# First attention of a fused kernel: tiles of 512 tokens, two changes of the array's form a group, and division by columns

## The chip, the cores and the metric

The kernel runs on one core of a Trainium2 chip, in one launch. The metric is the device time of that launch in microseconds, as the median of several executions. TensorE (PE) multiplies, VectorE (DVE), ScalarE (ACT) and GpSimd (POOL) do the elementwise work, SyncE (SP) issues the DMAs.

## What is computed

Attention in two steps over 32 inducing vectors, then two layers of a multilayer perceptron. N = 12480 tokens, C = 128, hidden width 2048:

```
def mab(q, kv):
    s = scale * (q @ kv.T);  s = s - s.max(-1)
    a = exp(s);  a /= a.sum(-1) + 1e-09
    return a @ kv
h = mab(inducing, x)                 # first attention: 32 x 128
x = mab(x, h)                        # second attention: 12480 x 128
h1 = x @ w_in;  g = maximum(h1, 0) + alpha * minimum(h1, 0);  x = g @ w_out
h2 = maximum(x @ w2_in, 0);  out = (h2 * h2) @ w2_out
```

The four weight matrices arrive as 64-bit floats and are turned into 32-bit floats on the chip, bit by bit.

## The kernel before, in words

The order of all work is written out by hand: each engine executes its instructions in the order of the program's lines, and SP issues the DMAs in that order too, with at most eight of them in flight.

**First attention** (lines 119 to 411). x is cut into 30 tiles of 416 tokens (104 partitions of 4 tokens), four tiles to a group, so that there are eight groups, the last of two tiles. `load_x(g)` (L119) loads a group in pairs of tiles, into four buffers `xg`. One turn of the loop (L332) does for group g:

- `scores` (L245): four matmuls against the inducing vectors, each on its own 32 columns of the array. Such matmuls use the array in another form than the full-width ones
- `transpose_x(g + 1)` (L231): 16 full-width transposes of the next group, into four PSUM banks; the copies to `xT` (L239) go to ACT and DVE in turn
- `maxima`, `exps`, `sums`: the running maximum on DVE (L268, L270), the exponentials on ACT (L280), the running sum
- `values1(g - 1)` (L303): 16 matmuls of 32 columns each; `add_values` adds them to `h_run`
- `transpose_e(g)` (L294): four full-width transposes of the exponentials, copied to `eT` by ACT (L301)
- one step of the conversion of a weight piece: `load_w` loads 512 KB into one of four buffers `raw`; `convs[k]` turns it into floats by two ACT instructions (L164, L167), two on DVE (L171, L175) and one on POOL (L176). Pieces 0 to 3 are `w_in`, 4 to 7 `w_out`

So the array changes its form four times a group. **The tail** (L367 to L415) ends the last group, brings the four running maxima together (L379 to L391), weighs the parts by `wgt` (L394), and makes `hT`, the transposed 32 x 128 result, as `h_run` times `sel` (L410). Here the sum of the weights is taken first, and its reciprocal goes into `sel` (L408):

```
    nc.vector.tensor_scalar(sel, same, wgt, den, op0=ALU.mult, op1=ALU.mult)
    b = y1_bank()
    nc.tensor.matmul(b[:, :P], h_run, sel, start=True, stop=True)
    nc.scalar.copy(hT, b[:, :P])
```

The four `transpose_w_in` (L360: four full-width transposes of `w_in`, then an ACT copy to `wiT`, L365) lie between these steps, and so does the vector `alpha` (L368 to L370).

**Start of the second part** (L514 to L535). `first` is the second attention of tile 0: scores (L432), a transposition on DVE (L440), maximum and difference (L445, L446), the exponentials on ACT (L449), sum, reciprocal, product (L454 to L458), back (L462), and a spread over partitions (L486, L493, L495). `make_w1s` multiplies `hT` by `w_in` (L505). The first matmul of the main loop (`l1_a`, L570) needs both.

**Main loop** (L718): 480 steps, one for each of 30 tiles and 16 pieces of 128 hidden units, with ten matmuls of 128 x 416 in a step. The conversions of `w2_in` and `w2_out`, the second attention of the later tiles, and the stores lie between the steps by a table (`plan`). The conversions follow at fixed steps, so the main loop starts when `hT` is there and works at a slower pace in its first steps.

Of the kernel before, what the change touches and what calls it, by code (L numbers as in the profile page):

```python
# [9 lines left out]
F32 = mybir.dt.float32  # L10
# [3 lines left out]
AF = mybir.ActivationFunctionType  # L14
ALU = mybir.AluOpType
AX = mybir.AxisListType

T, PT, R = 416, 104, 4  # L20

Q = 4

# [2 lines left out]
def attention_then_two_mlps(ctx: ExitStack, tc, x, inducing, w_in, w_out, alpha, w2_in, w2_out, out):  # L26
# [3 lines left out]
    nc = tc.nc  # L30
    _, N, C = x.shape
# [1 line left out]
    DFF = w_in.shape[1]  # L33
    P = 128
    NCH = DFF // P
    assert N % T == 0 and PT * R == T
    NT = N // T
    scale = 1.0 / math.sqrt(C)
    groups = [list(range(a, min(a + Q, NT))) for a in range(0, NT, Q)]

    keep = ctx.enter_context(tc.tile_pool(name="keep", bufs=1))
    att = ctx.enter_context(tc.tile_pool(name="att", bufs=1))
# [14 lines left out]
    def free_bank():  # L57
        turn[0] += 1
        return ms_bank() if turn[0] % 2 or main_loop else y2_bank()
# [13 lines left out]
    def st_tile(name, shape):  # L73
        return st.tile(shape, F32, name=name, tag=name)


    ident = st_tile("ident", [P, P])
    make_identity(nc, ident)

    same = st_tile("same", [P, P])  # L80
# [16 lines left out]
    def xt_cols(t):  # L97
        return xT[:, t * T : (t + 1) * T]
# [18 lines left out]
    x_t = {}  # L117

    def load_x(g):  # L119
        n = len(groups[g])  # L120
        t = st.tile([PT, Q, R, C], F32, name="xg", tag="xg", bufs=4)
        k = 2 if g and n > 1 else 1
        for a in range(0, n, k):
            t0 = groups[g][a]
            nc.sync.dma_start(
                out=t[:, a : a + k],
                in_=x[0, t0 * T : (t0 + k) * T, :].rearrange("(t p r) c -> p t r c", p=PT, r=R),
            )
            if g == a == 0:
                nc.sync.dma_start(out=ind, in_=inducing)  # L130
        x_t[g] = t
# [89 lines left out]
    for g in range(3):  # L221
        load_x(g)
    nc.sync.dma_start(out=al_raw, in_=alpha.rearrange("(c p) -> c p", p=P))
    load_w("w_in", 0)
    load_x(3)

# [1 line left out]

    def transpose_x(g):  # L231
        evac = []
        for i, t in enumerate(groups[g]):
            b = x_banks[i % 2]()
            for r in range(R):
                nc.tensor.transpose(b[:, r * PT : (r + 1) * PT], x_t[g][:, i, r, :], ident[:PT, :PT])  # L236
            copy = nc.vector.tensor_copy if i % 2 else nc.scalar.copy
            evac.append(
                lambda t=t, b=b, copy=copy: copy(  # L239
                    xt_cols(t).rearrange("c (p r) -> c p r", r=R), b[:, :T].rearrange("c (r p) -> c p r", r=R)  # L240
                )
            )
        return evac

    def scores(lhsT, tiles):  # L245
        b = free_bank()
        for i, t in enumerate(tiles):
            nc.tensor.matmul(
                b[i * M : (i + 1) * M, :T], lhsT, xt_cols(t), start=True, stop=True,
                tile_position=(0, i * M),  # L250
            )
        return b


    nm, e, f, s_g, eT, hb = {}, {}, {}, {}, {}, {}
    size = [len(tiles) * M for tiles in groups]
    last = len(groups) - 1

    def small(name):
        return att.tile([P, 1], F32, name=name, tag=name, bufs=2)  # L260
# [1 line left out]
    def maxima(g, b):  # L262
        n = size[g]
        top = small("top")
        nm[g] = small("nm")
        if n < P:
            nc.vector.tensor_copy(nm[g], nm[g - 1])
        nc.vector.reduce_max(top[:n], b[:n, :T], axis=AX.X)  # L268
        if g:
            nc.vector.scalar_tensor_tensor(  # L270
                nm[g][:n], top[:n], -scale, nm[g - 1][:n], op0=ALU.mult, op1=ALU.min
            )
        else:
            nc.vector.tensor_scalar_mul(nm[g][:n], top[:n], -scale)

    def exps(g, b):
        n = size[g]
        e[g] = st.tile([P, T], F32, name="e", tag="e", bufs=2)
        s_g[g] = small("s_g")
        nc.scalar.activation(e[g][:n], b[:n, :T], AF.Exp, bias=nm[g][:n], scale=scale, accum_out=s_g[g][:n])  # L280
# [12 lines left out]

    def transpose_e(g):  # L294
        n = size[g]
        b = y1_bank()
        own = e[g].rearrange("n (p r) -> n r p", r=R)
        for r in range(R):
            nc.tensor.transpose(b[:PT, r * P : r * P + n], own[:n, r], ident[:n, :n])
        eT[g] = st.tile([PT, R, P], F32, name="eT", tag="eT", bufs=2)  # L300
        nc.scalar.copy(eT[g][:, :, :n], b[:PT, : R * P].rearrange("p (r k) -> p r k", r=R)[:, :, :n])  # L301

    def values1(g):  # L303
        hb[g] = y2_bank()
        for r in range(R):
            for i in range(len(groups[g])):
                nc.tensor.matmul(
                    hb[g][i * M : (i + 1) * M, :C], eT[g][:, r, i * M : (i + 1) * M], x_t[g][:, i, r, :],
                    start=(r == 0), stop=(r == R - 1), tile_position=(0, i * M),
                )  # L310

    def add_values(g):
# [8 lines left out]
    def run(fs):  # L321
        for v in fs:
            v()
# [6 lines left out]
    nc.tensor.transpose(b[:, :M], ind, ident[:M, :M])  # L330
    nc.vector.tensor_copy(indT, b[:, :M])
    for g in range(last):  # L332
        cg = g - (last - 6)
        b = scores(indT, groups[g])
        evac = transpose_x(g + 1)
        maxima(g, b)
        evac[0]()
        exps(g, b)
        run(evac[1:2])
        if cg > 1:  # L340
            convs[cg - 2][2]()
        sums(g)
        if cg > 1:
            convs[cg - 2][3]()
        run(evac[2:])
        if cg > 0:
            run(convs[cg - 1][:2])
        if g:
            values1(g - 1)
            add_values(g - 1)  # L350
        transpose_e(g)
        if 0 <= cg < 3:
            load_w("w_in", cg + 1)
        elif cg >= 3:
            load_w("w_out", cg - 3)
        if g + 4 <= last:
            load_x(g + 4)
    load_w("w_out", 3)

    def transpose_w_in(k):  # L360
        b = x_banks[k % 2]()
# [5 lines left out]
    b = free_bank()  # L367
    nc.tensor.transpose(b[:, :NCH], al_raw, ident[:NCH, :NCH])  # L368
    nc.vector.tensor_copy(al, b[:, :NCH])
    nc.vector.tensor_scalar(al1, al, -1.0, 1.0, op0=ALU.mult, op1=ALU.add)  # L370


    b = scores(indT, groups[last])
    values1(last - 1)
    maxima(last, b)
    exps(last, b)
    add_values(last - 1)
    b = free_bank()
    nc.tensor.transpose(b[:1, :P], nm[last], ident)  # L379
    m_all = att.tile([1, M], F32, name="m_all", tag="m_all")  # L380
# [3 lines left out]
    convs[4][2]()  # L384
    sums(last)
    transpose_w_in(0)
    transpose_e(last)
    b = free_bank()
    nc.tensor.matmul(b[:, :1], m_rep.rearrange("o q j -> o (q j)"), ones[:1, :], start=True, stop=True)
    nb = att.tile([P, 1], F32, name="nb_all", tag="nb_all")  # L390
    nc.vector.tensor_copy(nb, b[:, :1])  # L391
    transpose_w_in(1)
    wgt = att.tile([P, 1], F32, name="wgt", tag="wgt")
    nc.scalar.activation(wgt, nm[last], AF.Exp, bias=nb, scale=-1.0)  # L394
    run(convs[5][:2])
    part = att.tile([P, 1], F32, name="part", tag="part")
    nc.vector.tensor_tensor(part, wgt, s_run, op=ALU.mult)
    convs[4][3]()
    values1(last)
    b = free_bank()  # L400
    nc.tensor.matmul(b[:, :1], same, part, start=True, stop=True)
    transpose_w_in(2)
    add_values(last)
    den = att.tile([P, 1], F32, name="den", tag="den")
    nc.vector.tensor_scalar_add(den, b[:, :1], 1e-9)
    nc.vector.reciprocal(den, den)
    sel = st.tile([P, P], F32, name="sel", tag="sel")
# [355 lines left out]
```

## Time and profile before

| | |
|---|---|
| median of 3 runs | 998.91 us (994.25 to 999.48) |
| the profiled execution | 999.72 us, of which the trace's span is 996.8 us |
| busy in the span | PE 98%, ACT 77%, DVE 69%, POOL 56% |
| mean granted TensorE clock | 0.993 of full speed |
| loads up to the main loop | x 6.39 MB, eight weight pieces of 512 KB |

Times in the trace are microseconds from the start of the span. A row of a timeline has start, duration, engine, line, operation, what it writes and reads, the shape and how many; the bracket at the end is the time in which the engine was idle before it, and what ended that. A chain of waits is followed back from the last instruction: each row is a piece of time and what held the kernel up in it.

### The profile page before, as it was taken

To read this page: it belongs to the slowest core of one execution; us is meant where nothing else is said; L and a number is where in the kernel's file an instruction comes from. 1 tells how busy PE (TensorE), PEld (TensorE's weight loads), DVE (VectorE), ACT (ScalarE), POOL (GpSimd) and SP (SyncE) were. 2 spreads that over 40 slices of the span, in tenths; PEclk is the share of its full clock that TensorE was granted. 3 is DMA by queue.
4 is the path that set the end of the run, shared out by engine and by line. 5 is a ranking of instruction groups with operands and counts; after the bars stand their busy time and mean duration, and the time that the engine had idled before them with its cause. 6 is when DMAs were issued, how large, how long until landed. Compare 5 with 4: busy or idle time off the path is not lost.

```text
span 996.8 us, 16261 instructions
## 1 busy us (share of the span) xinstructions
PE 973.7 (98%) x5423; PEld 939.9 (94%) x5423; DVE 684.8 (69%) x1210; ACT 770.4 (77%) x1607; POOL 555.3 (56%) x518
## 2 busy tenths in 40 slices
PE   7879999999999999999999999999999999999998
PEld 5558999999999999999999999999999999999997
DVE  4688776666766667666776667766677666776667
ACT  4569877777887778877787778877787777787776
POOL 1256966555665556655565555655556555565530
PEclk9889999999999999999999999999999999999999
DMA  8715002000020000100001000010000100010001
GB/s 220 200 56 149 1 9 44 10 7 4 10 44 10 10 1 10 44 10 10 3 10 42 10 9 10 10 35 10 9 9 18 27 10 9 10 27 1 10 9 18
DMA packets 66289, 28.42 MB, mean 29 GB/s; under 512 B 54205, under 2 KB 62061, under 8 KB 66205
## 3 DMA queue, kind: packets, MB, share of 16 engines
q1 hardware_dynamic: 66205, 27.39, 12.1%
q8 instruction: 42, 0.69, 0.3%
q14 instruction: 42, 0.34, 0.1%
HBM read 14.80 MB, written 6.39 MB: 21 GB/s over the span
## 4 chain that ended last, share of the span: by engine, by line
PE 91%; DMA 3%; DVE 2%; ACT 2%; issue 1%; POOL 0%; SPq 0%; ACTq 0%; POOLq 0%; DVEq 0%
PE y L582 18%; PE y L581 18%; PE y L580 17%; PE h L582 9%; PE h L581 9%; PE h L580 9%; PE h L570 9%; DMA xg<-in_x_dram 3%; PE ms L432 1%; PE y L597 1%; PE h L236 0%; DMA raw<-in_moe_w_out_dram 0%; ACT g1h L574 0%; DVE mag L175 0%; DVE g1l L576 0%
## 5 line engine op out<-in xcount | busy, mean ns | idle before, releaser
L622 POOL TENSOR_TENSOR g2l<-sq,g2h 128x416 fp32r<-128x416 f32 x456 | 496.2, 1089 | 343.9 <-ACT g2h L620 206.5
L576 DVE SCALAR_TENSOR_TENSOR g1l<-h,g1h 128x416 fp32r<-128x416 f32 x480 | 282.6, 589 | 221.7 <-ACT g1h L574 217.2
L574 ACT ACTIVATE g1h<-h 128x416 fp32r<-128x416 f32 x480 | 248.3, 518 | 132.9 <-PE h L570 129.9
L614 DVE TENSOR_TENSOR sq<-h,r 128x416 f32<-128x416 f32 x480 | 283.6, 591 | 52.2 <-ACT r L612 3.8
L612 ACT ACTIVATE r<-h 128x416 f32<-128x416 f32 x480 | 249.5, 520 | 53.6 <-PE h L582 7.7
L620 ACT CAST g2h<-sq 128x416 fp32r<-128x416 f32 x480 | 255.6, 532 | 2.3 <-DVE sq L614 2.1
L570 PE MATMUL h<-a_s,w1s 128*128 128x416 f32 (+1 forms) x480 | 170.4, 356 | 4.2 <-DVE g1l L576 2.9
L582 PE MATMUL y<-g2l,w2o_hi 128*128 128x416 f32 x480 | 168.7, 351 | 0.3 <-POOL g2l L622 0.3
L582 PE MATMUL y<-g1l,wo_hi 128*128 128x416 f32 x480 | 168.3, 351 | 0.0
L580 PE MATMUL h<-y1h,w2i_hi 128*128 128x416 f32 x480 | 168.1, 350 | 0.2
L582 PE MATMUL h<-y1l,w2i_hi 128*128 128x416 f32 x480 | 167.9, 350 | 0.2 <-DVE y1l L601 0.2
L581 PE MATMUL y<-g1h,wo_lo 128*128 128x416 f32 x480 | 168.0, 350 | 0.0
L581 PE MATMUL h<-y1h,w2i_lo 128*128 128x416 f32 x480 | 168.0, 350 | 0.0
L581 PE MATMUL y<-g2h,w2o_lo 128*128 128x416 f32 x480 | 168.0, 350 | 0.0
L580 PE MATMUL y<-g1h,wo_hi 128*128 128x416 f32 x480 | 167.7, 349 | 0.0
L580 PE MATMUL y<-g2h,w2o_hi 128*128 128x416 f32 x480 | 167.5, 349 | 0.0
L570 PEld LDWEIGHTS h<-a_s,w1s 128*128 128x128 f32 (+1 forms) x480 | 90.5, 189 | 12.0 <-DVE g1l L576 5.7
L580 PEld LDWEIGHTS h<-y1h,w2i_hi 128*128 128x128 f32 x480 | 90.0, 188 | 2.8 <-DVE sq L614 1.4
L580 PEld LDWEIGHTS y<-g1h,wo_hi 128*128 128x128 f32 x480 | 90.3, 188 | 1.0 <-issue 0.5
L582 PEld LDWEIGHTS y<-g2l,w2o_hi 128*128 128x128 f32 x480 | 90.1, 188 | 1.2 <-POOL g2l L622 0.7
L581 PEld LDWEIGHTS y<-g2h,w2o_lo 128*128 128x128 f32 x480 | 90.1, 188 | 0.9 <-POOL w2o_lo L181 0.3
L581 PEld LDWEIGHTS y<-g1h,wo_lo 128*128 128x128 f32 x480 | 90.3, 188 | 0.5
(127 smaller groups left out, 761.4 us busy)
## 6 DMA issues: line engine op xcount, KB each, us to landing
out_dram<-o SPq DMA_DIRECT2D x120, 52.0 KB
xg<-in_x_dram SPq DMA_DIRECT2D x13, 416.0 KB
raw<-in_moe_w_in_dram SPq DMA_DIRECT2D x8, 512.0 KB
raw<-in_moe_w_out_dram SPq DMA_DIRECT2D x8, 512.0 KB
a_s<-a_hi SPq DMA_DIRECT2D x58, 52.0 KB
a_s<-a_lo SPq DMA_DIRECT2D x58, 52.0 KB
xg<-in_x_dram SPq DMA_DIRECT2D x4, 208.0 KB
ind<-in_inducing_dram SPq DMA_DIRECT2D x1, 16.0 KB
```

Of the source, the lines that this page charges most:

```text
L432: nc.tensor.matmul(b[i * M : (i + 1) * M, :w], hT[:, :M], rhs, start=True, stop=True, tile_position=(0, i * M),)
L570: nc.tensor.matmul(b[:, :T], w1s[: a.shape[0], c * P : (c + 1) * P], a, start=True, stop=True)
L574: nc.scalar.activation(hi, b[:, :T], AF.Relu)
L576: nc.vector.scalar_tensor_tensor(lo, b[:, :T], 0.0, f32(hi), op0=ALU.max, op1=ALU.subtract)
L580: nc.tensor.matmul(b, w_hi, hi, start=start, stop=False)
L581: nc.tensor.matmul(b, w_lo, hi, start=False, stop=False)
L582: nc.tensor.matmul(b, w_hi, lo, start=False, stop=stop)
L597: nc.tensor.matmul(b, v_s[: a.shape[0]], a, start=False, stop=True)
L612: nc.scalar.activation(r, b, AF.Relu)
L614: nc.vector.tensor_tensor(sq, b, r, op=ALU.mult)
L620: nc.scalar.copy(hi, sq)
L622: (nc.vector if i >= total - LAG2 else nc.gpsimd).tensor_tensor(lo, sq, f32(hi), op=ALU.subtract)
```

## The change

The first attention gets tiles of its own: 24 tiles of 512 tokens (128 partitions of 4) and one of 192 (96 partitions of 2), that is six full groups and a last one of one tile. The second attention and the main loop keep their tiles of 416.

- **Loads.** `load_x` runs three groups ahead instead of four, and the four `w_in` pieces are issued before the loop, between the groups of x. The `w_out` pieces follow in the loop
- **One turn of the loop.** The ACT part of the conversion comes first, then `scores(g)` and `values1(g - 1)` together (the 32-column matmuls), then maximum and exponentials, then the transposes of x and of e together (the full-width ones). The copies to `xT` come at once behind the transposes
- **Alpha** moves from the tail into the third turn; the conversion of the first `w_out` piece ends inside the loop
- **The tail.** `sel` holds the weights alone. A second matmul gives the denominators as columns (L405 of the changed kernel), and the copy of `hT` becomes a product with their reciprocals on DVE (L413). The copy of the joint maximum (`nb_all`) is gone: ACT reads it from PSUM
- **The `w_in` transposes.** Two stay in the tail, the third moves behind `first[0]`, the fourth behind `second[0]`; they use the `y2` banks
- **Buffers.** `ident` moves to another pool, since it lives longer, and a small tile is made wider, so that the main loop's buffers stay at their addresses

The core of the diff:

```diff
+TILE1 = (512, 128, 4)
+REST1 = (192, 96, 2)
...
+    load_x(0)
+    load_x(1)
+    load_w("w_in", 0)
+    load_x(2)
+    load_w("w_in", 1)
     nc.sync.dma_start(out=al_raw, in_=alpha.rearrange("(c p) -> c p", p=P))
-    load_w("w_in", 0)
     load_x(3)
+    load_w("w_in", 2)
+    load_w("w_in", 3)
...
-            copy = nc.vector.tensor_copy if i % 2 else nc.scalar.copy
+            copy = nc.scalar.copy if i in (0, 3) else nc.vector.tensor_copy
...
     for g in range(last):
...
+        if g:
+            run(convs[g - 1][:2])
+        b = scores(g)
         if g:
             values1(g - 1)
+        maxima(g, b)
+        exps(g, b)
+        if g:
             add_values(g - 1)
+            convs[g - 1][2]()
+        run(transpose_x(g + 1))
         transpose_e(g)
...
+        sums(g)
+        if g:
+            convs[g - 1][3]()
+        if 0 < g and g + 3 <= last:
+            load_x(g + 3)
+        if 0 < g <= 4:
+            load_w("w_out", g - 1)
...
-    nc.vector.tensor_scalar(sel, same, wgt, den, op0=ALU.mult, op1=ALU.mult)
+    nc.vector.tensor_scalar(sel, same, wgt, None, op0=ALU.mult)
+    values1(last)
+    run(convs[5][:2])
+
+    d = ms_bank()
+    nc.tensor.matmul(d[:, :M], s_run.to_broadcast([P, P]), sel[:, :M], start=True, stop=True)
+    add_values(last)
+    den = st.tile([P, M], F32, name="den", tag="den")
+    nc.vector.tensor_scalar_add(den, d[:, :M], 1e-9)
+    nc.vector.reciprocal(den, den)
     transpose_w_in(0)
...
     b = y1_bank()
     nc.tensor.matmul(b[:, :P], h_run, sel, start=True, stop=True)
-    nc.scalar.copy(hT, b[:, :P])
-    transpose_w_in(3)
-    stage1.close()
+    nc.vector.tensor_tensor(
+        hT.rearrange("c (q j) -> c q j", q=Q), b[:, :P].rearrange("c (q j) -> c q j", q=Q),
+        den.unsqueeze(1).to_broadcast([P, Q, M]), op=ALU.mult,
+    )
+    transpose_w_in(1)
...
     make_w1s(0)
+    transpose_w_in(2)
     run(convs[6][:2])
     run(first[1:4])
     split_w1s(0, 0)
     second[0]()
+    transpose_w_in(3)
+    stage1.close()
     make_w1s(1)
```

PE from the last transposes of x to the product that gives `hT`, before (names as in the text; `h_` and `y_` with a number are PSUM banks):

```order
L236 MATMUL h_586<-ident,xg 128x104 x4
L307 MATMUL y_609<-xg,eT 32x128 x16
L299 MATMUL y_627<-ident,e 104x128 x4
L368 MATMUL ms<-ident,al_raw 128x16
L248 MATMUL y_642<-xT,indT 32x416 x2
L307 MATMUL y_645<-xg,eT 32x128 x16
L379 MATMUL ms<-ident,nm 1x128
L364 MATMUL h_681<-ident,w_in_sb 128x128 x4
L299 MATMUL y_687<-ident,e 104x64 x4
L389 MATMUL y_694<-ones,m_rep 128x1
L364 MATMUL h_698<-ident,w_in_sb 128x128 x4
L307 MATMUL y_713<-xg,eT 32x128 x8
```

and with the change:

```order
L248 MATMUL h_556<-ident,xg 128x96 x2
L312 MATMUL y_560<-ident,e 128x128 x4
L260 MATMUL ms<-xT,indT 32x192
L321 MATMUL y_572<-xg,eT 32x128 x16
L385 MATMUL y_599<-ident,nm 1x128
L312 MATMUL y_601<-ident,e 96x32 x2
L392 MATMUL ms<-ones,m_rep 128x1
L321 MATMUL y_620<-xg,eT 32x128 x2
L405 MATMUL ms<-sel,s_run 128x32
L376 MATMUL y_632<-ident,w_in_sb 128x128 x4
L412 MATMUL y_638<-sel,h_run 128x128
```

The last group has one tile of 192 instead of two of 416, and one block of `w_in` transposes stands before the last product where three stood.

ACT from `hT` to the first copy for the main loop (L493 / L497), before:

```order
L411 COPY hT<-y_736 128x128
L365 COPY wiT<-h_739 128x512
L164 ACTIVATE mag<-raw 128x512
L167 ACTIVATE raw<-raw 128x512
L449 ACTIVATE a_760<-a_760 128x128
L512 CAST w1s<-h_755 128x512
L200 CAST wo_hi<-aw 128x512
L493 CAST a_s<-y_784 96x416
```

and with the change:

```order
L377 COPY wiT<-y_641 128x512
L377 COPY wiT<-y_658 128x512
L172 ACTIVATE mag<-raw 128x512
L175 ACTIVATE raw<-raw 128x512
L453 ACTIVATE a_667<-a_667 128x128
L516 CAST w1s<-h_656 128x512
L377 COPY wiT<-y_678 128x512
L208 CAST wo_hi<-aw 128x512
L497 CAST a_s<-y_698 96x416
```

`hT` leaves this queue (DVE writes it), and two more `wiT` copies enter it, one of them ahead of the exponentials of the first tile.

## Rows read from the trace of the kernel before

**Rows 1.** The page: the chain that ended last, share of the span by engine.

```profile
PE 91%; DMA 3%; DVE 2%; ACT 2%; issue 1%; POOL 0%; SPq 0%; ACTq 0%; POOLq 0%; DVEq 0%
```

**Rows 2.** The chain of waits in order of time: start, duration, what.

```profile
2.44 4.34 DMA xg<-in_x_dram
...
27.07 9.68 DMA xg<-in_x_dram
...
36.88 1.62 PE h L236 x8
38.50 1.87 PE y L307 x32
40.36 1.03 PE y L299 x4
41.40 1.55 PE y L248 x8
...
46.16 1.08 DVE al L370
...
52.51 0.96 DVE sel L408
```

**Rows 3.** Windows: stretch, length, busy time of each engine, PE clock, DMA share, GB/s.

```profile
4.00:8.00 4.00, 2.97 (x16) 2.22 (x14) 1.57 (x6) 1.01 (x2) 0.00 (x0) 1.00 0.82 236
...
20.00:30.00 10.00, 8.51 (x120) 5.86 (x120) 5.95 (x16) 7.36 (x19) 1.30 (x1) 1.00 0.97 247
30.00:40.00 10.00, 7.40 (x100) 5.65 (x100) 5.13 (x12) 5.08 (x14) 2.60 (x2) 0.82 0.96 237
...
57.00:63.00 6.00, 3.57 (x15) 1.83 (x13) 5.25 (x11) 3.29 (x7) 3.62 (x4) 1.00 0.23 83
64.00:70.00 6.00, 4.91 (x10) 3.38 (x11) 5.73 (x12) 3.91 (x8) 3.68 (x3) 0.50 0.00 0
```

**Rows 4.** Timeline of the last two groups and the tail, 43 to 53 us.

```profile
43.09 0.59 DVE L268 TENSOR_REDUCE top<-y 128x1 f32<-128x416 f32 x1 [2.31 <-PE y L248]
...
44.05 0.61 ACT L280 ACTIVATE e<-y,nm 128x416 f32<-128x416 f32 x1
44.51 0.41 DVE L171 TENSOR_SCALAR mag<-mag 128x512 int32<-128x512 int32 x1
...
44.91 0.69 PE L299 MATMUL y<-ident,e 128*104 128x128 f32 x4
...
45.10 0.68 DVE L175 SCALAR_TENSOR_TENSOR mag<-raw,mag 128x512 int32<-128x512 int32 x1
...
48.04 0.27 PE L379 MATMUL ms<-ident,nm 128*1 128x128 f32 x1 [0.34 <-DVE nm L270]
...
49.38 0.38 PE L389 MATMUL y<-ones,m_rep 1*128 1x1 f32 x2
...
50.87 0.30 ACT L394 ACTIVATE wgt<-nm,nb_all 128x1 f32<-128x1 f32 x1
...
52.09 1.29 POOL L176 TENSOR_TENSOR w_out_sb<-mag,raw 128x512 int32<-128x512 int32 x1 [4.88 <-DVE mag L175]
```

**Rows 5.** Timeline around the end of the first attention, 53 to 58 us.

```profile
53.90 0.60 PE L364 MATMUL h<-ident,w_in_sb 128*128 128x128 f32 x4
54.10 0.27 ACT L411 COPY hT<-y 128x128 f32<-128x128 f32 x1 [1.13 <-PE y L410]
...
54.54 0.58 ACT L365 COPY wiT<-h 128x512 f32<-128x512 f32 x1 [0.17 <-PE h L364]
...
54.79 1.13 PE L505 MATMUL h<-w_in_sb,hT 128*128 128x512 f32 x2
...
55.02 0.69 ACT L164 ACTIVATE mag<-raw 128x512 f32<-128x512 f32 x1
...
56.16 0.32 ACT L449 ACTIVATE a<-a 128x128 f32<-128x128 f32 x1
...
57.26 0.87 DVE L458 TENSOR_TENSOR a<-a,sm 128x128 f32<-128x128 f32 x1
```

More of the change, by code (lines that the diff above doesn't have):

```diff
@@ L35, in attention_then_two_mlps @@
     NCH = DFF // P
-    assert N % T == 0 and PT * R == T
+    assert N % T == 0
     NT = N // T
@@ L39, in attention_then_two_mlps @@
     groups = [list(range(a, min(a + Q, NT))) for a in range(0, NT, Q)]
+    n1, rest1 = divmod(N, TILE1[0])
+    assert rest1 == REST1[0] and n1 % Q == 0
+    tiles1 = [(i * TILE1[0], *TILE1) for i in range(n1)] + [(n1 * TILE1[0], *REST1)]
+    groups1 = [tiles1[a : a + Q] for a in range(0, len(tiles1), Q)]
     keep = ctx.enter_context(tc.tile_pool(name="keep", bufs=1))
@@ L119, in load_x @@
     def load_x(g):
[L120 to L124, printed above, removed]
+        _, n, p, r = groups1[g][0]
+        t = st.tile([P, Q, TILE1[2], C], F32, name="xg", tag="xg", bufs=4)
+        k = 2 if g else 1
+        for a in range(0, len(groups1[g]), k):
+            t0, kk = groups1[g][a][0], min(k, len(groups1[g]))
             nc.sync.dma_start(
-                out=t[:, a : a + k],
-                in_=x[0, t0 * T : (t0 + k) * T, :].rearrange("(t p r) c -> p t r c", p=PT, r=R),
+                out=t[:p, a : a + kk, :r],
+                in_=x[0, t0 : t0 + kk * n, :].rearrange("(t p r) c -> p t r c", p=p, r=r),
             )
@@ L232, in transpose_x @@
         evac = []
[L233 removed]
+        for i, (t0, n, p, r) in enumerate(groups1[g]):
             b = x_banks[i % 2]()
[L235 to L237 removed]
+            for k in range(r):
+                nc.tensor.transpose(b[:, k * p : (k + 1) * p], x_t[g][:p, i, k, :], ident[:p, :p])
+            copy = nc.scalar.copy if i in (0, 3) else nc.vector.tensor_copy
             evac.append(
[L239 to L240 removed]
+                lambda t0=t0, n=n, r=r, b=b, copy=copy: copy(
+                    xT[:, t0 : t0 + n].rearrange("c (p r) -> c p r", r=r), b[:, :n].rearrange("c (r p) -> c p r", r=r)
                 )
@@ L243, in transpose_x, with scores @@
         return evac
-    def scores(lhsT, tiles):
-        b = free_bank()
-        for i, t in enumerate(tiles):
+    def scores(g):
+        b = ms_bank()
+        for i, (t0, n, _, _) in enumerate(groups1[g]):
             nc.tensor.matmul(
-                b[i * M : (i + 1) * M, :T], lhsT, xt_cols(t), start=True, stop=True,
+                b[i * M : (i + 1) * M, :n], indT, xT[:, t0 : t0 + n], start=True, stop=True,
                 tile_position=(0, i * M),
             )
-        return b
+        return b[:, :n]
     nm, e, f, s_g, eT, hb = {}, {}, {}, {}, {}, {}
-    size = [len(tiles) * M for tiles in groups]
-    last = len(groups) - 1
+    size = [len(tiles) * M for tiles in groups1]
+    last = len(groups1) - 1
     def small(name):
@@ L332, in attention_then_two_mlps @@
     for g in range(last):
[L333 to L347, printed above, removed]
+        if g:
+            run(convs[g - 1][:2])
+        b = scores(g)
         if g:
             values1(g - 1)
+        maxima(g, b)
+        exps(g, b)
+        if g:
             add_values(g - 1)
+            convs[g - 1][2]()
+        run(transpose_x(g + 1))
         transpose_e(g)
[L352 to L358, printed above, removed]
+        sums(g)
[5 more added lines that the diff above has]
+            load_w("w_out", g - 1)
+        if g == 2:
+            b = y2_bank()
+            nc.tensor.transpose(b[:, :NCH], al_raw, ident[:NCH, :NCH])
+            nc.vector.tensor_copy(al, b[:, :NCH])
+            nc.vector.tensor_scalar(al1, al, -1.0, 1.0, op0=ALU.mult, op1=ALU.add)
     def transpose_w_in(k):
-        b = x_banks[k % 2]()
+        b = y2_bank()
         for i in range(4):
@@ L365, in transpose_w_in @@
         nc.scalar.copy(wiT[:, k * 512 : (k + 1) * 512], b)
[L367 to L373, printed above, removed]
+    b = scores(last)
     values1(last - 1)
@@ L383, in attention_then_two_mlps @@
     nc.vector.tensor_copy(m_rep, m_all.unsqueeze(1).to_broadcast([1, Q, M]))
-    convs[4][2]()
+    b = ms_bank()
+    nc.tensor.matmul(b[:, :1], m_rep.rearrange("o q j -> o (q j)"), ones[:1, :], start=True, stop=True)
+    add_values(last - 1)
     sums(last)
-    transpose_w_in(0)
[L387 to L407, printed above, removed]
-    nc.vector.tensor_scalar(sel, same, wgt, den, op0=ALU.mult, op1=ALU.mult)
+    nnm = att.tile([P, 17], F32, name="nnm", tag="nnm")[:, :1]
+    nc.vector.tensor_scalar_mul(nnm, nm[last], -1.0)
+    wgt = att.tile([P, 1], F32, name="wgt", tag="wgt")
+    nc.scalar.activation(wgt, b[:, :1], AF.Exp, bias=nnm)
+    sel = st.tile([P, P], F32, name="sel", tag="sel")
+    nc.vector.tensor_scalar(sel, same, wgt, None, op0=ALU.mult)
[7 more added lines that the diff above has]
+    nc.vector.reciprocal(den, den)
+    transpose_w_in(0)
     b = y1_bank()
     nc.tensor.matmul(b[:, :P], h_run, sel, start=True, stop=True)
-    nc.scalar.copy(hT, b[:, :P])
-    transpose_w_in(3)
-    stage1.close()
+    nc.vector.tensor_tensor(
[3 more added lines that the diff above has]
+    transpose_w_in(1)
     run(convs[5][2:4])
```

36 lines of the change are left out of this document (18 added, 18 removed).

## The prediction

> **What bounds the kernel now.** I read the chain of waits first, by engine [rows 1]: 91% of it is PE. That is the main loop, whose matmuls the diff leaves alone, and whose buffers it keeps where they were. So the change can only move the moment at which the main loop starts. The chain in order of time says what sets that moment [rows 2]. Up to 36.75 us (27.07 + 9.68) the last piece is a transfer of x, so the first attention waits for data and not for an engine. Behind it comes a chain through PE, DVE and ACT that ends with `hT`, written at 54.37 (54.10 + 0.27) [rows 5]. The windows give the rate at which the data come [rows 3]: 236 to 247 GB/s. [...]
>
> Of the main loop one thing counts: whether it follows a shift one for one. Its first steps hang on `hT` through the same order of instructions on ACT, DVE and POOL as before, and the later conversions are tied to steps and not to times. I carry the shift to the end without loss.
>
> **Term 1: when the last full group of x has landed.** Before, that is group 6 of 0 to 7. Ahead of its end lie 28 tiles of 212,992 bytes and three weight pieces of 524,288, 7.54 MB. Now it is group 5 of 0 to 6: 24 tiles of 262,144 bytes and five pieces (all of `w_in` and one of `w_out`), 8.91 MB. The first bytes move at 2.44 [rows 2]. At 237 GB/s [rows 3] 8.91 MB take 37.6 us and land at 40.0; at 247 GB/s [rows 3] they take 36.1 us and land at 38.5; and if a busy share of 0.97 could become 1.00, at 255 GB/s, they land at 37.4. Against 36.75 this is later by 3.3, 1.8 or 0.6. I take 1.2, the middle of the last two, since they come from the stretch with nearly all engines busy, and that is what all of the new stage looks like. The rest of the loop is not on this path: PE works 8.51 of 10 us for 120 instructions, two groups [rows 3], so 4.3 us a group and 5.2 with tiles of 512, while a group of 1.05 MB with a weight piece takes 6.4 us to load at 247 GB/s. On SP the `w_out` piece ahead of group 5 waits for POOL's conversion of the first `w_in` piece, which lands by 13 us, so it holds nothing up. On ACT the conversion steps now stand ahead of the exponentials; the second and third `w_in` piece land behind their groups, which may hold a turn up by 2 us, and the wait for the next group takes that in.
>
> There is a way below 0.6. Between 4 and 8 us, when only x moves, the engines are busy for 0.82 of their time and carry 236 GB/s [rows 3]. 13 of 16 is 0.81, and 104 partitions split into 13 equal parts of 8, 128 into 16. [...] If each engine kept its pace, 16 would carry 236 / 0.82 = 288 GB/s, and the group would land at 33.4. The row from 20 to 30 speaks against that: at 0.97 the engines carry 247, not 279. So I make it a rival, and the term stays at +1.2.
>
> **Term 2: from that landing to `hT`.** Before: 54.37 - 36.75 = 17.6 us. Now, counted from the landing, at the clock of the rows before:
>
> - Eight transposes of 128 columns: 1.62 x 128/104 = 2.0 [rows 2], ends at 2.1 with the gap of 0.13. The transposes of e, 1.03 [rows 2], cover the last copy: 3.1. Four scores of 512 columns: 1.55 x 512/416 = 1.9 [rows 2]: 5.0.
> - Maximum 0.59 x 512/416 = 0.73 [rows 4], with gaps and the small `nm` behind it 6.0. Exponentials 0.61 x 512/416 = 0.75 [rows 4] and the reading of their sums: 6.9. Transposes of e 0.69 [rows 4]: 7.7.
> - DVE has in between the sum of the values, two conversion steps of 0.41 and 0.68 [rows 4] and a running sum. The values of group 4 end on PE at about 6.9 (1.87 behind the scores [rows 2]); these four take 1.7: 8.6. The maximum of the one small tile and two small instructions: 9.2 (an estimate: 0.59 x 192/416 and two of 0.15).
> - PE makes the values of group 5 from 8.35 on, 1.0 (half of 1.87, the clock is back): 9.4. Then `nm` is turned, 0.27 [rows 4]: 9.7. Joint minimum and its copy, 0.5 (an estimate, two small DVE instructions of some 0.25): 10.2. Broadcast 0.38: 10.6. `wgt` 0.30: 10.9 [rows 4].
> - `sel`: it took 0.96 [rows 2], and ended 0.1 behind POOL's conversion (52.09 + 1.29 = 53.38) [rows 4]; without POOL it should cost at most 0.41, as another TENSOR_SCALAR of DVE over 512 columns does [rows 4]. In the new tail POOL's conversion starts at 8.6 and is done at 9.9, so: 11.3.
> - The small matmul of denominators, 0.3; four transposes of `w_in`, 0.60 [rows 5]; the product, 0.46 (an estimate from these); the division on DVE, 0.4 (the copy that it replaces took 0.27): with gaps, `hT` at 13.2.
>
> The gain is 17.6 - 13.2 = 4.4 us. It comes from three places: the alpha instruction (1.08 [rows 2]) out of the way, the last group of one small tile, and fewer transposes and steps between the maximum and the product. The parallel work (denominators, reciprocal) hides behind the transposes of `w_in`; without them it would cost some 0.4.
>
> **Term 3: from `hT` to the main loop.** Here the change costs. The exponentials of the first tile (L449) ended at 56.16 + 0.32 = 56.48 [rows 5], 2.1 behind `hT`. Now ACT has a `wiT` copy ahead of them whose transposes stand on PE behind `make_w1s`. Sum: scores 0.5, L505 1.13, transposes 0.60, copy 0.58, the two conversion steps 0.69 and 0.6, exponentials 0.32 [rows 5]: 4.4, so 2.3 later. Back comes part of the product L458, 0.87 for 128 columns [rows 5], which like `sel` stood in POOL's time; I take 0.4. The fourth block of transposes and its copy lie in time in which ACT waits for the spread on PE (0.60 and 0.58), and I cost them at nothing; if that cover were gone they would cost 0.6. Net +1.9.
>
> **Two changes of form a group instead of four** I cost at nothing: in the loop PE waits for x anyway. At most it is worth the gap of 0.13 us that PE shows ahead of a block [rows 2], twice in the tail.
>
> **The sum** is +1.2 - 4.4 + 1.9 = -1.3 us on the profiled execution's 999.72, that is 998.4. That execution stands 0.8 above the median, so I forecast 997.6 as the median. A measurement of this kernel can tell some 0.5% (5.0 us) from no change, and -1.3 is inside that.
>
> **The rivals.**
>
> - **The clock stays up.** PE fell to half clock twice: after its wait for x, and after 57 to 63, where it was busy for 3.57 of 6 us [rows 3]. From 64 to 70 PE is busy for 4.91 us at 0.50 [rows 3]; at full clock half of that, 2.4 us, is saved. The earlier stretch holds 6.07 us of PE pieces [rows 2], 3.0 at full clock. The two extra transpose blocks behind `hT` make PE busier there, which speaks for it; PE still waits for x, which speaks against the first. One stretch gone: 995.2 (0.20). Both gone: 992.2 (0.07).
> - **Sixteen engines at the pace of thirteen.** Term 1 becomes -3.4 instead of +1.2: 993.0. For it: 0.82 at 236 GB/s. Against it: 247 at 0.97 (0.14).
> - **The bytes set the pace, and there are more of them ahead of the last full group.** The loads come at 237 GB/s or less, since two more weight pieces were moved ahead of it. At 237 the sum is +3.3 - 2.5 = +0.8: 999.7, slower than before. It decides when the group lands later than 39.2; slower by over 0.5% it is only from 44.2 on, a rate of 213 GB/s, which no row shows (0.10 for slower at all, 0.04 of it past the bound, with a third slow stretch of the clock).
> - **The forecast** as it stands: 0.49.
>
> **How the numbers follow.** Faster by over 0.5% (under 993.9) needs both clock stretches gone, or sixteen engines at full pace: 0.21 in all, with a little from one stretch gone and a landing at 37.4, 0.23. Slower by over 0.5%: 0.04. The rest, 0.73, is within 0.5%. The range goes from 991.5, which takes in both ways to be faster, to 1000.5, the pace of 237 GB/s and some tenths of error in terms 2 and 3; what lies outside is the two ways together, and a late landing with a further clock stretch.
>
> **What would show it.** In the profile of the changed kernel the last full group of x should end between 37 and 39 us, `hT` some 13 us later, at about 51, and the first L577 about 8.3 behind `hT`, where it was 6.5. `sel` should take under 0.45. If the group lands before 35, the engines kept their pace. If the first main-loop matmul comes earlier by some 1.3 us but the end moves by another amount, the shift is not carried one for one, and the theory of the main loop is wrong. If no low clock shows behind 55, the clock explains the rest.

## The result and the profile after

The changed kernel takes 987.01 us (median of 4 runs, 985.42 to 988.19) against 999.1 for the kernel before, measured beside it: ratio 0.9889, 95% interval [0.9855, 0.9923]. Measured again it was 986.72 against 997.77, ratio 0.9879 [0.9859, 0.9899]. The forecast of 997.6 and its range from 991.5 were wrong: the gain is 12 us, not 1.3. The profiled execution has a span of 983.6 us (before 996.8).

The page of the changed kernel, first the chain that ended last by engine, then the rate of the DMAs in 40 slices:

```profile
PE 94%; DVE 2%; ACT 2%; DMA 1%; issue 0%; POOL 0%; SPq 0%; ACTq 0%; DVEq 0%
GB/s 329 147 101 55 10 11 34 10 10 10 15 30 10 10 9 18 27 10 10 10 21 25 10 9 10 23 23 10 9 9 30 16 10 10 10 27 1 10 9 19
```

DMA was 3% of the chain [rows 1] and is 1% now: the waits for x have left it. Windows of the changed kernel (columns as in [rows 3]):

```profile
4.00:8.00 4.00, 3.07 (x14) 2.27 (x13) 2.17 (x6) 0.59 (x1) 0.00 (x0) 1.00 0.95 289
12.00:16.00 4.00, 4.00 (x56) 3.02 (x54) 2.22 (x7) 3.60 (x10) 0.00 (x0) 1.00 1.04 403
20.00:24.00 4.00, 4.00 (x60) 3.13 (x58) 3.29 (x9) 3.51 (x8) 1.23 (x1) 1.00 1.06 377
...
28.00:30.00 2.00, 2.00 (x29) 1.80 (x20) 1.63 (x5) 1.65 (x5) 0.56 (x1) 1.00 0.43 119
```

Where 236 to 247 GB/s moved before [rows 3], 289 to 403 move now, and by 28 us the first rush of loads is over. In the windows from 12 and from 20 on PE is busy for all of the 4.00 us. The chain of waits in order of time shows the same:

```profile
2.60 4.85 DMA xg<-in_x_dram
...
15.07 1.90 PE h L248 x16
16.96 0.48 PE y L312 x4
17.44 1.09 PE ms L260 x8
18.53 1.03 PE y L321 x31
...
28.54 1.90 PE h L248 x16
30.43 0.48 PE y L312 x4
30.91 1.26 PE ms L260 x8
```

Behind 7.5 us no load of x stands in it (before, the last one ended at 36.75 [rows 2]). From 10 to 31 us the stage is PE alone, 1.90 + 0.48 + 1.09 + 1.03 = 4.5 us a group. The second load of the last full group completes at 28.75 in the trace, when PE has just begun, at 28.54, to transpose that group's first tiles. The timeline of the end of the first attention and of what follows (it answers to [rows 4, 5]):

```profile
35.63 0.82 DVE L282 SCALAR_TENSOR_TENSOR nm<-top,nm 32x1 f32<-32x1 f32 x1
...
38.27 0.29 DVE L400 TENSOR_SCALAR sel<-same,wgt 128x128 f32<-128x128 f32 x1 [0.39 <-ACT wgt L398]
...
39.75 0.29 DVE L413 TENSOR_TENSOR hT<-y,den 128x128 f32<-128x128 f32 x1
...
43.77 0.30 ACT L453 ACTIVATE a<-a 128x128 f32<-128x128 f32 x1
...
44.84 0.29 DVE L462 TENSOR_TENSOR a<-a,sm 128x128 f32<-128x128 f32 x1
...
47.84 0.84 PE L577 MATMUL h<-a_s,w1s 96*128 96x416 f32 x3 [1.23 <-DVE a_s L499]
```

`hT` ends at 40.04 instead of 54.37 [rows 5], the first main-loop matmul (L577) starts at 47.84 instead of 60.83. From there to the end both take 936 us (935.8 and 936.0).

### The profile page after: what moved, and what is told of

Its sections match the earlier page's. It is cut to its first block, busy times and chain, and to the rows that moved or that the text cites. A ratio compares the mean times of both kernels' runs of the same rounds, so it can differ in the third digit from the quotient of the medians.

```text
span 983.6 us, 16078 instructions
## 1 busy us (share of the span) xinstructions
PE 965.0 (98%) x5341; PEld 936.8 (95%) x5341; DVE 683.1 (69%) x1203; ACT 768.5 (78%) x1600; POOL 555.1 (56%) x518
## 4 chain that ended last, share of the span: by engine, by line
PE 94%; DVE 2%; ACT 2%; DMA 1%; issue 0%; POOL 0%; SPq 0%; ACTq 0%; DVEq 0%
PE y L589 18%; PE y L588 18%; PE y L587 18%; PE h L587 9%; PE h L589 9%; PE h L588 9%; PE h L577 9%; PE h L248 1%; PE ms L260 1%; PE ms L436 1%; PE y L604 1%; ACT g1h L581 1%; PE y L321 1%; DMA xg<-in_x_dram 0%; DVE g1l L583 0%
## 5 line engine op out<-in xcount | busy, mean ns | idle before, releaser
L577 PE MATMUL h<-a_s,w1s 128*128 128x416 f32 (+1 forms) x480 | 170.0, 355 | 4.5 <-DVE g1l L583 2.8
L577 PEld LDWEIGHTS h<-a_s,w1s 128*128 128x128 f32 (+1 forms) x480 | 90.1, 188 | 12.5 <-DVE g1l L583 6.1
L589 PEld LDWEIGHTS h<-y1l,w2i_hi 128*128 128x128 f32 x480 | 90.0, 188 | 0.7 <-DVE y1l L608 0.5
```

Source lines behind the costliest of these rows:

```text
L577: nc.tensor.matmul(b[:, :T], w1s[: a.shape[0], c * P : (c + 1) * P], a, start=True, stop=True)
L589: nc.tensor.matmul(b, w_hi, lo, start=False, stop=stop)
```

## The experiments

**The two halves of the change, each alone.** First the changed kernel with tiles of 416 tokens (the new order, forms and division stay):

```
-TILE1 = (512, 128, 4)
-REST1 = (192, 96, 2)
+TILE1 = (416, 104, 4)
...
-        if g:
+        if 0 < g < 6:
             run(convs[g - 1][:2])
```

> The changed kernel with its first attention back on tiles of 416 tokens (104 partitions); order of the loop, loads between the groups and the new tail stay. Theory A, the gain comes from loading x on 128 partitions: x comes at some 240 GB/s again, hT is written after 48 us, and the time is 994 to 1000 us. Rival B, the gain comes from the order (two changes of form, tail, alpha): hT by 43 us, 986 to 990 us.

Measured: 1002.31 us, ratio to before 1.0040 [1.0021, 1.0059]. The order, the forms and the division without the larger tiles bring no gain; the run is slower. Loads of x are back on its chain (12.76, 11.77 and 9.33 us long), and `hT` ends at 52.05, 2.3 us earlier than before. The main loop starts at 60.96, though, where it was 60.83: from `hT` to there it takes 8.91 instead of 6.46. The changed kernel takes 7.80 there; in this run the clock is at 0.50 from 51 to 54 besides (mean 0.83 from 50 to 60), and the `make_w1s` in that time takes 1.64 instead of 1.06. (The profiled execution took 998.82, the shortest of ten, so its trace does not show all of what the median lost.)

Then the kernel before with nothing but the tiles of 512:

```
-T, PT, R = 416, 104, 4
+T = 416
+TILE1 = (512, 128, 4)
+REST1 = (192, 96, 2)
...
-        t = st.tile([PT, Q, R, C], F32, name="xg", tag="xg", bufs=4)
+        t = st.tile([P, Q, TILE1[2], C], F32, name="xg", tag="xg", bufs=4)
```

> The kernel before with tiles of 512 tokens in the first attention and nothing else changed (its order of loop, loads and tail). Theory A: x comes at over 350 GB/s, hT by 44 us, 987 to 992 us. Rival B: hT after 50 us, 996 us or more.

Measured: 992.43 us, 0.9949 [0.9932, 0.9967]. Here, too, no load of x stands on the chain behind 5.4 us; `hT` ends at 45.85. So the tiles gain 6 us in the old order and 15 in the new one, while the new order loses 4 us with the old tiles and gains 5 with the new ones. The change is not the sum of its parts. With tiles of 416 both orders end the scores of the last full group at nearly the same time (42.95 before, 42.56 in the first of these runs), and what the new order gains from there to `hT` is lost behind it. With tiles of 512 the new order ends them at 32.17 or 33.83 in two executions, the old one at 34.85, and the stretch from there to `hT` is 3.1 us shorter.

**The speed of the loads alone.** Tiles of 512 also change PE's work and the number of groups. This kernel keeps all of the change and only issues each load of x over 128 partitions as two:

```
-            nc.sync.dma_start(
-                out=t[:p, a : a + kk, :r],
-                in_=x[0, t0 : t0 + kk * n, :].rearrange("(t p r) c -> p t r c", p=p, r=r),
-            )
+            src = x[0, t0 : t0 + kk * n, :].rearrange("(t p r) c -> p t r c", p=p, r=r)
+            for u, v in [(0, 104), (104, 128)] if p == P else [(0, p)]:
+                nc.sync.dma_start(out=t[u:v, a : a + kk, :r], in_=src[u:v])
```

> The changed kernel, tiles of 512 tokens and all, with every load of x over 128 partitions issued as two, 104 and 24 partitions, which the loads alone moved at 246 GB/s (0.89 of the engines' time) where one load over 128 moved 388. Nothing else changes. Theory (what the changed kernel gained is the speed of its loads, and without it the 8.91 MB ahead of the last full group set the end as predicted): windows at 230 to 265 GB/s, the first stage waits for x again, the last full group lands 36 to 40 us, hT at 46 to 52 us, 992 to 999 us. Rival (fewer groups, two forms a group and the new end make the gain, and the loads only fill what is free): 986 to 988.5 us.

Measured: 1001.97 us, 1.0028 [1.0011, 1.0045]. A window of it, and the loads on its chain in order of time:

```profile
20.00:30.00 10.00, 7.04 (x70) 5.13 (x69) 4.25 (x9) 4.36 (x9) 1.30 (x1) 0.83 0.97 233
```

```profile
4.87 7.34 DMA xg<-in_x_dram
...
12.23 11.67 DMA raw<-in_moe_w_in_dram
...
23.98 11.23 DMA xg<-in_x_dram
...
35.23 10.33 DMA xg<-in_x_dram
```

The rate is that of before or a little less (233 GB/s here, 247 in the same window before), the last full group lands at 45.55, `hT` ends at 56.34, and the whole gain is gone, with some 3 us more. It was slower than I expected (992 to 999; the bytes that Term 1 left out, below, are the likely reason), but the rival, 986 to 988.5, is out: the gain needs the fast loads. The split also doubles the number of loads. That two loads a tile are not slow of themselves is shown further down, where two loads onto every second partition reach 384 GB/s.

**Why loads over 128 partitions are faster.** Four kernels of loads alone, 2 KB a packet, one stage after the other. In the first, loads over 104, 128, 96, 112, 104 (tiles 512 tokens apart), 120 and 128 (tiles 544 apart) partitions:

```
+    for name, p, step in [("p104", 104, 416), ("p128", 128, 512), ("p96", 96, 384), ("p112", 112, 448),
+                          ("p104_at_512", 104, 512), ("p120", 120, 480), ("p128_at_544", 128, 544)]:
+        stage(name, p, step)
```

> Leaves out the whole computation: it loads x again and again in pairs of tiles, with 104, 128, 96, 112, 104, 120 and 128 partitions a tile, and writes zeros to 128 rows of the output. [...]

Windows of it, one in each of the first four stages and in the last three (columns: stretch, length, DVE, POOL, clock, DMA share, GB/s):

```profile
6.00:16.00 10.00, 0.00 (x0) 0.00 (x0) 1.00 0.86 218
34.00:42.00 8.00, 0.00 (x0) 0.00 (x0) 1.00 1.05 384
52.00:60.00 8.00, 0.00 (x0) 0.00 (x0) 1.00 1.05 282
66.00:80.00 14.00, 0.17 (x1) 0.00 (x0) 1.00 1.07 254
92.00:102.00 10.00, 0.17 (x1) 0.00 (x0) 1.00 0.87 208
114.00:130.00 16.00, 0.17 (x1) 0.00 (x0) 1.00 1.00 230
146.00:152.00 6.00, 0.17 (x1) 0.00 (x0) 1.00 1.03 379
```

The distance of the tiles in memory plays no part (218 and 208; 384 and 379). Nor does the busy share of the engines decide: at 96, 112 and 120 partitions it is 1.00 or more, with 282, 254 and 230 GB/s, and at 128 it is 1.05 and 1.03, with 384 and 379. At 128 the packets take less time. Share x 16 engines x 2048 bytes / rate gives 129 ns a packet at 104 partitions, 122 at 96, and 90 at 128. The second kernel takes other counts and splits:

```
+        ("p64", 256, [(0, 64)]),
+        ("p32", 128, [(0, 32)]),
...
+        ("p64_40", 416, [(0, 64), (64, 104)]),
...
+        ("p104_24", 512, [(0, 104), (104, 128)]),
+        ("p64_64", 512, [(0, 64), (64, 128)]),
```

> Leaves out all of the computation: loads of x alone into eight buffers, stage by stage: 128 partitions in one load, 64, 32, 104 in one load, 104 as 64+40, as 64+32+8, 128 as 104+24, 128 as 64+64. Theory A (the partition count of a whole load decides how its 2 KB packets are dealt to the engines, and 128, 64 and 32 are dealt evenly): 64, 32 and 64+64 reach 340 to 400 GB/s as 128 does, and 104 as 64+32+8 over 300. Theory B (only loads over all 128 partitions are fast, since then each engine keeps to partitions of its own): 64, 32 and 64+64 stay at 220 to 290 GB/s, as 96 and 112 did. Either way 128 as 104+24 should fall to 210 to 260 GB/s, since its large part is the load of 104 partitions.

Its windows for 128, 64, 32 and 104 partitions, and for 128 as 104 + 24 and as 64 + 64 (104 in pieces gave 224 and 242):

```profile
8.00:16.00 8.00, 0.00 (x0) 0.00 (x0) 1.00 1.05 388
24.00:36.00 12.00, 0.00 (x0) 0.00 (x0) 1.00 1.07 202
42.00:48.00 6.00, 0.00 (x0) 0.00 (x0) 1.00 0.99 186
54.00:74.00 20.00, 0.00 (x0) 0.00 (x0) 1.00 0.90 203
...
134.00:154.00 20.00, 0.00 (x0) 0.00 (x0) 1.00 0.89 247
162.00:176.00 14.00, 0.00 (x0) 0.00 (x0) 1.00 1.06 282
```

Theory A falls: 64 and 32 partitions are as slow as 104. Theory B's rates are the nearer ones, though 64 and 32 lie below its 220; and 104 + 24 is slow (247), as both said. To which partitions an engine keeps, no run shows. The third kernel asks whether the count or the place of the partitions matters, by loads onto every second and every fourth partition:

```
+        ("p64_of_128", 256, [slice(0, 128, 2)]),
...
+        ("halves", 512, [slice(1, 128, 2), slice(0, 128, 2)]),
+        ("p32_of_128", 128, [slice(0, 128, 4)]),
```

> Leaves out all of the computation: loads of x alone, stage by stage, over 128 partitions, the first 64, every second partition (64 of 128), the first 104, 128 as two loads of every second partition, every fourth (32 of 128), the first 112, and 128 again. Theory (what counts is over how much of the buffer's 128 partitions the engines write at once, so that packets to the same stretch of partitions slow each other): every second partition reaches 340 to 400 GB/s where the first 64 stay at 202, every fourth over 300. Rival (the count of a load decides, wherever its partitions lie): every second partition stays at 190 to 290 GB/s. Both: 128 at 385, 104 at 205 to 217, 112 at 255.

Its windows for the first 64, every second, and 128 as two loads of every second:

```profile
24.00:35.00 11.00, 0.00 (x0) 0.00 (x0) 1.00 1.07 213
40.00:46.00 6.00, 0.00 (x0) 0.00 (x0) 1.00 1.04 375
...
81.00:91.00 10.00, 0.00 (x0) 0.00 (x0) 1.00 1.04 384
```

For every second partition the theory's rate is there: 64 partitions are fast when they are spread over the whole buffer (375) and slow when they are its first half (213), with the engines busy at 1.04 and 1.07. (Every fourth partition gave 204, where the theory had over 300, with the engines busy for 0.69 in a stage of under 7 us; the next run has it with larger loads.) In the same run 112 partitions reached 299 GB/s, so that rate varies. The fourth kernel:

```
+        ("at_0_32", [slice(0, 32), slice(32, 64)], 4),
+        ("at_0_64", [slice(0, 32), slice(64, 96)], 4),
...
+        ("every_4th", [slice(0, 128, 4)], 4),
+        ("every_2nd", [slice(0, 128, 2)], 4),
```

> Leaves out all of the computation: loads of x alone, stage by stage, 2 KB a packet: over 128 partitions, over 32 (0 to 31), over two times 32 in two loads (0 to 31 and 32 to 63), over two times 32 that lie 64 apart (0 to 31 and 64 to 95), over four times 32 in four loads, every fourth partition, every second, and the first 104. [...] Theory B (the wider the partitions are spread the faster, by distance alone): 0 and 32 together lie clearly above 32 alone, and 0 and 64 not above 0 and 32 by more than a third. Theory C (the count of partitions in a load decides): 0 and 32 as fast as 0 and 64, both near 203, the run with every second partition notwithstanding. [...]

Windows for 0 to 31, 0 and 32 together, 0 and 64 together, four loads of 32, every fourth, and every second:

```profile
25.00:39.00 14.00, 0.00 (x0) 0.00 (x0) 1.00 1.07 199
45.00:66.00 21.00, 0.00 (x0) 0.00 (x0) 1.00 1.07 209
74.00:92.00 18.00, 0.00 (x0) 0.00 (x0) 1.00 1.07 246
100.00:118.00 18.00, 0.00 (x0) 0.00 (x0) 1.00 1.07 228
125.00:132.00 7.00, 0.00 (x0) 0.00 (x0) 1.00 0.91 294
138.00:148.00 10.00, 0.00 (x0) 0.00 (x0) 1.00 1.05 391
```

Neither theory holds whole. By B, 0 and 32 together should lie clearly above 32 alone; they lie 5% above it (209 against 199), while 0 and 64 lie 18% above them (246). C had both pairs near 203, which 246 is not. Every fourth partition reaches 294, with the engines busy for 0.91, and four narrow loads that fill all 128 partitions reach only 228. What is shown is that 32 partitions in a row are about as slow as 64 (186 and 199 for 0 to 31, 202 and 213 for 0 to 63), that 64 are fast in one load that is spread (375 and 391) and slow in one that is not, and that narrow loads in flight together mend only a part (282 for 0 to 63 with 64 to 127, against 202 for one of them). The engines are busy at 1.07 in a narrow load and at 1.05 in one over every second partition, so what differs is the time of a packet, 174 ns (at 202 GB/s) against 88 (at 391); what makes it longer, no run shows. Why 96, 104, 112 and 120 lie where they do stays open too.

**The smaller terms.** The changed kernel again, beside its variants:

> The changed kernel once more, beside the variants that follow, on the same chip. Both theories: 0.989 of the kernel before, 987 us. Beyond that it fixes how far two executions of one program differ up to hT: the clock's first rise at 9 to 15 us after the span's start moves hT between 40.0 and 42.5 us.

Measured: 986.72, and `hT` at 41.68 in this execution instead of 40.04. The first pieces of its chain say why:

```profile
9.71 1.96 PE ms L260 x8
11.67 2.45 PE h L248 x16
```

In the first profile these scores took 1.13 and the transposes 1.90. The first record of a full granted clock stands at 8.67 us there and at 12.78 here, behind the scores and part of the transposes. (Ahead of that record the trace has none, and a window reads 1.00 there. That TensorE did not yet have its full clock there is read from these rows: 1.96 for the scores here against 1.08 for those of the next group.) From the last scores to `hT` both took 7.9 us.

The old division, the weights divided before the product:

```
+    nc.vector.tensor_scalar(sel, same, wgt, den, op0=ALU.mult, op1=ALU.mult)
...
-    nc.vector.tensor_tensor(
-        hT.rearrange("c (q j) -> c q j", q=Q), b[:, :P].rearrange("c (q j) -> c q j", q=Q),
-        den.unsqueeze(1).to_broadcast([P, Q, M]), op=ALU.mult,
-    )
+    nc.scalar.copy(hT, b[:, :P])
```

> The changed kernel with the old end of the first attention: the weights are divided before the last product (part, one column of same x part, sel = same*wgt*den, plain copy of hT by ACT) and not h in its columns. Theory (the new division takes sel and its 0.96 us off the chain into hT): hT 0.7 to 1.2 us later than in the changed kernel's run beside it, 988 us. Rival (hT is set by the product of the last values and its sum into h_run, or the conversions on DVE, so the division lies beside it): within 0.3 us of the changed kernel, 987 us.

Measured: 988.06, 0.9892 [0.9871, 0.9913], not to be told from the changed kernel by the time alone. In the trace the way from the last full group's scores to `hT` is 8.42 us (32.24 to 40.66) instead of 7.87: the new division is worth some 0.5 us, between the two expectations. Every run with the new division and tiles of 512 has 7.85 to 7.87 there. Two pieces of its chain:

```profile
14.43 10.39 DMA xg<-in_x_dram
...
39.41 0.36 DVE sel L411
```

`sel` with both factors costs 0.36 here, and not the 0.96 of [rows 2], which lay in the time of POOL's conversion (52.09 to 53.38 [rows 4]). And in this execution, whose clock rose earlier (its first scores took 1.17), the stage waited for x once, up to 24.81: the loads are only just ahead of PE.

Four changes of the form a group, as before:

```
-        if g:
-            values1(g - 1)
         maxima(g, b)
...
         run(transpose_x(g + 1))
+        if g:
+            values1(g - 1)
+            add_values(g - 1)
         transpose_e(g)
```

> The changed kernel with the values of the group before moved behind the transposes of the next group's x, as in the kernel before: the form of the array changes four times a group instead of twice. Theory (the first stage is PE's now, so each change counts in full; the run with 512-token tiles in the old order shows the transposes of e at 0.68 us where the changed kernel shows 0.48): 0.1 to 0.25 us a group, 0.6 to 1.5 us in six groups, 988 us. Rival (a change costs nothing that another engine does not hide, or the new place lets ACT and DVE evacuate sooner): within 0.3 us, 987 us.

Measured: 988.27, 0.9897 [0.9874, 0.9921]. From the start of group 1's scores to the end of group 5's it takes 19.93 us (15.00 to 34.93), the changed kernel beside it 19.23 (14.60 to 33.83): 0.7 us in all, at the low end of what I expected. The times alone do not tell the two apart. One turn of it:

```profile
16.26 1.90 PE h L248 x16
18.16 1.01 PE y L321 x32
19.17 0.68 PE y L312 x4
19.85 1.00 PE ms L260 x8
```

The transposes of e take 0.68 behind the narrow matmuls and 0.48 behind other transposes.

The third block of `w_in` transposes moved out of the way of the first exponentials:

```
 make_w1s(0)
-transpose_w_in(2)
...
 second[0]()
+transpose_w_in(2)
 transpose_w_in(3)
```

> The changed kernel with its third block of w_in transposes moved behind second[0], next to the fourth, so that no wiT copy stands between hT and the exponentials of the first tile. Theory, the way from hT to the first matmul of the main loop is what the prediction said in term 3, and the main loop follows one for one: 2 us shorter (some 6 instead of 8.1), 984 to 985.5 us. Rival, the first steps of the main loop are bound by ACT's or SP's work, and the shift is lost: 986.5 to 987.5 us.

Measured: 986.45, 0.9887 [0.9854, 0.9919]. The exponentials end 2.97 us behind `hT` instead of 4.03, but the main loop starts 7.37 behind it instead of 7.80, so over half of that is lost on the way: the product behind them (L462) starts while POOL still converts and takes 0.87 again, where the changed kernel had 0.29, with POOL idle from 44.57 to 45.62. Neither expectation had that, and in the time the rest can't be seen.

Eight transposes more, before x arrives:

```
     make_identity(nc, ident)
+    b = y1_bank()
+    for i in range(8):
+        nc.tensor.transpose(b[:, :P], ident, ident)
```

> The changed kernel with eight transposes of ident by itself ahead of the first of x, in the time in which TensorE has nothing to do (until 3.5 us). Theory (TensorE sets the first stage and works at the half clock until 8.7 to 14 us in different executions, 1.90 or 2.45 to 3.6 us for the first sixteen transposes): the clock rises before the first scores in every execution, hT 39.5 to 40.5 us, 985.5 us, 0 to 2 us better than the changed kernel. Rival (the landing of x is next: in the run with the old division the clock rose at 7 us and the stage waited for x at 24.8): hT 40 us and no later gain, 986.5 us. Second rival (the eight transposes delay the first of x): 0.5 us slower, 987.5 us.

Measured: 986.88, 0.9873 [0.9854, 0.9893]. The first record of a full clock stands at 12.73 us, the second group's transposes take 2.67 us (1.90 and 2.45 in the two executions above), and `hT` ends at 41.41: eight transposes did not bring the clock up earlier, and the theory falls. No version here beats the changed kernel by more than the measurement can tell.

## Why the prediction was wrong

| Step | Predicted | Measured |
|---|---|---|
| landing of the last full group | 37.95 | 28.75 |
| end of its scores | 42.95 | 32.17 |
| from there to `hT` | 8.2 | 7.87 |
| `hT` to the end of the first exponentials | 4.4 | 4.03 |
| `hT` to the first main-loop matmul | 8.3 | 7.80 |
| from there to the end | 936.0 | 935.8 |

- **Term 1 is the step that failed.** It had the landing of the last full group 1.2 us later than before; it came 8.0 us earlier. The end of that group's scores, 42.95 before and by the forecast, came at 32.17, 10.8 us earlier. I took the rates in [rows 3] for a property of the chip; they were a property of loads over 104 partitions. The share of 0.97 at 247 GB/s, by which I turned down the rival, is time in which packets last, not work: the same engines carry 391 GB/s at 1.05 when the load is spread. The run with split loads shows it: the same bytes in the same order at 233 GB/s give 1001.97 us.
- **Term 1 also counted too few bytes**, and this error went the other way. By the same sum the kernel before would have landed its 7.54 MB at 33.0 to 34.2, and [rows 2] has 36.75. At the 240 GB/s that its trace shows from 2.44 to 36.75, 8.2 MB had moved by then. I read the difference of 0.7 MB as loads issued behind that group, which take a part of the engines' time before it is complete. I set a sum without them against a landing with them. An estimate that adds the 1.38 MB more at 247 GB/s to 36.75 makes the term +5.6 and the sum +3.1; the two runs with slow loads were slower by 3.8 and 3.4 us, and with split loads the group landed at 45.55. So -1.3 was not right for the old rate either.
- **The rival "sixteen engines at the pace of thirteen"** was right in its direction and had 0.14. Its 288 GB/s is what the window from 4 to 8 shows (289 at 0.95), but behind it the engines got faster too, 377 to 403. How many engines a load over 104 partitions uses, and that it is thirteen, no run shows; the busy share of the sixteen was 0.82 in that window before [rows 3] and 0.86 to 0.91 where such loads ran alone. So even its landing at 33.4 and its 993.0 were too late.
- **The loop's own pace.** I had put a group of PE's work at 5.2 us and cost it at nothing behind 6.4 us of loading. It is 4.5 us, and now it is the bound, since 1.57 MB (a group with a weight piece) take 3.9 to 4.2 us at 377 to 403 GB/s: 28.54 + 1.90 + 0.48 + 1.26 makes the end of the scores, whatever lands earlier.
- **"The bytes set the pace, and there are more of them"** did not come true here, but in the two runs with slow loads the new order is slower than before, 1.0040 and 1.0028.
- **Term 2 held in mechanism and nearly in size**: 8.2 us behind the scores, 7.87 measured; `sel` 0.29, as foretold under 0.45. In the kernel before with tiles of 512 that stretch is 11.0 us (34.85 to 45.85), so the new order is worth 3.1 in it (0.3 of that is the last product, which takes 0.77 there instead of 0.46, in ten us with a mean clock of 0.71). One piece I had not seen: the small `nm` takes 0.82 instead of 0.15 to 0.18, in time in which POOL converts (35.14 to 36.44). The first 5.0 us of the term, from the landing to the end of the scores, were priced at half clock and can't be read in the changed kernel, where PE no longer waits for the landing; with split loads they were 2.9, its eight transposes 1.06 of that, the pace of full clock (1.90 for sixteen).
- **Term 3**: +1.9 foretold, +1.3 measured (6.5 to 7.8). The copy of `wiT` ahead of the first exponentials is there as described (4.4 foretold, 4.03); the product gave back 0.58 instead of 0.4.
- **The forms at nothing**: wrong once PE does not wait for x, 0.7 us in the run that undoes them. No run takes them alone where PE waits.
- **The main loop carries the shift one for one**: 935.5 to 936.9 us from its first matmul to the end in every profile above.
- **The clock**: of the two low stretches of the rival "the clock stays up", the first, behind the wait for x (mean 0.82 from 30 to 40 [rows 3]), is gone with that wait, 1.00 in all windows up to 40; in the trace of before it was 0.50 from 36.4 to 43.2. Where the loads are slow, a low clock is back (0.83 from 20 to 30 us and 0.78 from 30 to 40 in the run with split loads, 0.83 from 30 to 40 with tiles of 416). So the rival came true in part, as a result of what Term 1 had wrong, and its 3.0 us are not to be added to the 10.8. The second stretch is still there behind `hT`, 0.50 from 53.0 to 56.5 (before, 63.7 to 70.6), so the last sign that I had set, no low clock behind 55, did not come. The mean from 50 to 60, 0.83 here, was 0.66 with the third block of `w_in` moved, in a run of the same time, so the length of this stretch says nothing of the change. A window of the changed kernel that holds it:

```profile
50.00:60.00 10.00, 7.65 (x28) 6.29 (x29) 9.57 (x18) 7.64 (x19) 5.78 (x5) 0.83 0.02 5
```

Against the forecast the measured terms are 10.8 us earlier at the end of the scores, 0.3 shorter to `hT`, 0.6 to the main loop (7.80 for 6.46 + 1.9) and 0.2 behind it: 11.9 us, by which the span's -13.2 (983.6 against 996.8) missed the -1.3.

## What to carry to other kernels

A measured DMA rate belongs to the shape of the loads that gave it: before it is used for a load of another shape, ask over which partitions one load is spread, and let a load of 0.97 busy engines prove no ceiling. Here one load over all 128 partitions, or over every second of them, moved 375 to 403 GB/s once the first loads were under way (every fourth 294), one over 64 or 104 in a row about 200 to 250. A sum of bytes for a landing should be tried on the kernel before first: here 8.2 MB had moved at a landing for which the sum had 7.54. When a wait goes, everything that was hidden in it gets a price (here the array's forms and PE's own 4.5 us a group), so the next bound has to be worked out and not only the old one moved.

## What was unexpected of the hardware

- 64 partitions in a row load at 202 to 213 GB/s, 64 in every second place at 375 to 391, at nearly the same busy share (1.07 against 1.04 and 1.05): 165 to 174 ns against 88 to 91 ns a packet of 2 KB.
- More partitions were slower in several cases: 96 gave 282 GB/s, 112 gave 254 and 299, 120 gave 230, 104 between 203 and 245.
- Splitting a fast load of 128 into 104 + 24 costs a third of the rate (247 instead of 388), into 64 + 64 a quarter (282), into every second partition nothing (384).
